# Splitting the attention values: scaled in place on ScalarE, their low halves subtracted on GpSimd from the fifth head on

## Chip, core and metric

One core of one Trainium2 chip runs the whole kernel. The metric is the device time of an execution in microseconds (us), from three timed runs; a profile of one more execution shows what each engine did.

## What is computed

Three layers follow each other. The change lies in the first.

```
# attention, 2 batches x 8 heads, 768 positions, 64 columns a head
q_bits = (q @ proj > 0); k_bits = (k @ proj > 0)      # 6 bits: a bucket for each row
mask   = q_bucket[:, None] == k_bucket[None, :]
scores = where(mask, q @ k.T / 8, -1e9)
out    = softmax(scores) @ v
# mixture of experts: 1536 tokens, each to its best of 8 experts, capacity 384
# last: g = h * clip(h + 3, 0, 6) / 6 with h = x @ w_in, and then g @ w_out
```

## The kernel before

**Precision.** Most products run in float16. A float32 number is split in two: a high half, which is the number scaled and rounded to float16, and a low half, which is the scaled number minus the high half, again rounded to float16. A product is the sum of high by high, high by low and low by high. The values `v` are split so by `vsplit(h)`, one head at a time. Their scale `s` is a power of two which the kernel finds for every group of four heads (`vmax`, `vscale`), so that scaling doesn't round.

**Attention.** The sixteen heads are cut into 96 steps, six a head, each with 128 keys and all 768 queries. For a step, `scores` makes two products on TensorE for each half of the queries, into a buffer `pst` of PSUM (L442 and L443; two such buffers), and ScalarE writes their exponentials to `pf` (L444). A step later `phi` takes the high half of `pf` (`high`, L452 on ScalarE; for a few steps L454 on VectorE), and a step after that `plo` its low half (`low`, L458, on GpSimd for steps below 84 and two later ones, otherwise on VectorE). `pv` multiplies both with the values of the head, two steps at a time, four and five steps behind the scores (L470 to L472); it reads the tile `vh` that `vsplit` writes. Eight steps ahead of the scores, `mx` makes products `psm` (L425, three buffers) of which VectorE takes the row maximum (L428).

**Around a head.** `prep` splits queries and keys (`hi` by ScalarE, L359; `lo` by VectorE, L375). `vgate` multiplies values with the expert gate on TensorE (L531) and VectorE splits the result into other columns of `vh` (L540, L541). `bits` makes the bucket bits (L398 and L387). `evac` divides a finished head by its sum (L480 to L488), and `tally` adds up the logits (L503 and L507, mostly on GpSimd).

**Order.** Nothing is scheduled by the compiler: each engine runs its instructions in the order in which the program issues them. The loop over steps issues the regular work; everything else is entered in a table `later` under a due step, and `due(k)` issues it. `spread(k, gen)` runs a generator up to its next `yield` once every step. So the first part of `vsplit(h)` is issued at step 6h plus an offset (-3.25, -4.75, -1.75 or -2.25 by the head's place in its group; heads 0 to 3 have steps of their own: 2, 3.75, 4 and 16.25), and its second part one step later. Loads of values (`load_v`) go through SyncE's queue into one of two `vr` tiles, each of which holds four heads.

**After attention.** At the end of attention the last steps' `plo`, the first expert's weight splits (`wh` by ScalarE, L157; `wl` by VectorE, L163) and the routing (`route`, `weigh`) share VectorE. Then the tokens are gathered through HBM, and the experts and the last layer follow, which the change doesn't touch.

Of the kernel before, what the change touches and what calls it, by code (L numbers as in the profile page):

```python
# [13 lines left out]
AF = mybir.ActivationFunctionType  # L14
ALU = mybir.AluOpType
# [5 lines left out]
B, H, S, D = 2, 8, 768, 64  # L21
# [19 lines left out]
VA = DE + 1  # L41
# [22 lines left out]
def moe_attention_kernel(ctx, tc, qk, v, vt, pj, wg, w1, w2, win, wout, out, cap):  # L64
    nc = tc.nc
    pe, act, dve, pool, sp = nc.tensor, nc.scalar, nc.vector, nc.gpsimd, nc.sync
# [3 lines left out]
    def opened(stack, name, bufs, side="left", **kw):  # L70
        return stack.enter_context(tc.tile_pool(name=name, bufs=bufs, side=side, reuse_waits="tile", **kw))
# [232 lines left out]
    with ExitStack() as actx:  # L304
# [361 lines left out]
        def vh(h):  # L666
            if h not in vh_t:
                vh_t[h] = pt.tile([P, NC, VW], F16, tag="vh", name=f"vh{h}", bufs=4)
            return vh_t[h]

        def vsplit(h):
            g = h // 4
            r = vr_t[g][:, h % 4]
            s = sc_t[g][:, 0:1]
            t = vh(h)
            o = E * (1 - h % 2)
            act.activation(t[:, :, o : o + D], r, AF.Copy, scale=s)
            yield
            dve.scalar_tensor_tensor(
                out=t[:, :, VA + o : VA + o + D], in0=r, scalar=s, in1=t[:, :, o : o + D],  # L680
                op0=ALU.mult, op1=ALU.subtract,
            )
            dve.memset(t[:, :, DE:VA], 1.0)

# [99 lines left out]
        for h in range(NH):  # L784
            spread(Q["v4"][h] if h < 4 else NC * h + Q["v"][h % 4], vsplit(h))
# [54 lines left out]
        h = NH - 1  # L840
# [242 lines left out]
    def heat(n):  # L1083
# [21 lines left out]
        out=gates, in0=ps2[:, :, NW:], scalar=1.0 / LS, in1=gates, op0=ALU.mult, op1=ALU.add  # L1105
# [239 lines left out]
    with ExitStack() as octx:  # L1345
        op = opened(octx, "op", 1)
# [127 lines left out]
```

## Time and profile before

| | |
|---|---|
| three runs, median | 677.33 us (677.24 to 678.81) |
| profiled execution | 675.88 us |
| its span, first to last instruction | 674.1 us |
| mean granted TensorE clock | 0.981 |
| busy over the span: TensorE, VectorE, ScalarE, GpSimd | 638.4, 481.0, 426.6, 229.8 us |
| attention | until about 240 us of the span |

The span is shorter than the execution by 1.8 us, which lie before its first and after its last instruction. Times within a trace count from the start of the span. TensorE's busy time includes matrix products that wait in its pipeline, so a busy TensorE is not one at its peak. Engines have the names PE (TensorE), PEld (its weight loads), DVE (VectorE), ACT (ScalarE), POOL (GpSimd) and SP (SyncE).

### The profile page before, as it was taken

The page shows a single profiled execution, that of the slowest core. Times are in us where ns is not written, and L with a number is a line of the kernel's source. Part 1 is how long each engine was busy: PE and PEld are TensorE (multiplying, and loading weights), DVE is VectorE, ACT ScalarE, POOL GpSimd, SP SyncE. Part 2 cuts the span into 40 slices and gives each one's busy share as a digit, 9 for nine tenths or more (in the row PEclk, how much of TensorE's full clock was granted, in tenths as well). Part 3 has the DMA queues.
Part 4 walks back from the last instruction along what each step waited for, and adds up shares of the span by engine and source line. Part 5 has one row for each costly group of instructions (what it writes and reads, how often), then busy time and mean ns, then how long its engine had stood idle before and what let it go on. Part 6 is the DMA issues. An engine that isn't in the chain of part 4 may idle for free.

```text
span 674.1 us, 14367 instructions
## 1 busy us (share of the span) xinstructions
PE 638.4 (95%) x5518; PEld 479.7 (71%) x5518; DVE 481.0 (71%) x1038; ACT 426.6 (63%) x869; POOL 229.8 (34%) x199
## 2 busy tenths in 40 slices
PE   7899999999999769999999999999999999999894
PEld 2588889989899638999999997555555555555541
DVE  6768898898999957888888877888888452222320
ACT  3467778778787826776667765455445576555730
POOL 4339769769778233221077500000000021000011
PEclk9889999999999978999999999999999999999998
DMA  8584764764465065777677735443442011000011
GB/s 236 127 233 115 231 177 122 233 169 109 126 160 165 25 217 193 250 246 257 213 253 228 243 115 162 137 145 126 150 134 92 0 48 48 1 0 1 1 41 59
DMA packets 37840, 94.14 MB, mean 140 GB/s; under 512 B 7576, under 2 KB 13720, under 8 KB 37760
## 3 DMA queue, kind: packets, MB, share of 16 engines
q1 hardware_dynamic: 34672, 85.71, 42.7%
q0 software_dynamic: 2400, 7.36, 3.2%
q8 instruction: 46, 0.75, 0.4%
q14 instruction: 34, 0.28, 0.1%
q10 hardware_dynamic: 688, 0.03, 0.1%
HBM read 67.14 MB, written 6.29 MB: 109 GB/s over the span
## 4 chain that ended last, share of the span: by engine, by line
PE 75%; DVE 10%; DMA 6%; ACT 5%; issue 2%; SPq 0%; POOL 0%; POOLq 0%; ACTq 0%; DVEq 0%
PE psg L1249 16%; PE pso L1276 15%; PE psh L1006 11%; PE psy L1033 11%; PE psm L425 5%; PE pst L442 4%; PE pst L443 3%; DVE mx L428 2%; DMA out_dram<-os,inv 2%; PE psv L470 2%; PE psv L471 2%; PE psv L472 2%; PE psg L531 2%; DMA vr<-in_v_dram 1%; ACT junk L1203 1%
## 5 line engine op out<-in xcount | busy, mean ns | idle before, releaser
L458 POOL TENSOR_TENSOR plo<-pf,phi 128x768 f16<-128x768 f32 x86 | 147.1, 1736 | 60.4 <-ACT phi L452 24.9
L444 ACT ACTIVATE pf<-pst 128x384 f32<-128x384 f32 x192 | 83.5, 486 | 47.4 <-PE pst L443 45.7
L428 DVE TENSOR_REDUCE mx<-psm 128x1 f32<-128x384 f32 x192 | 96.3, 548 | 20.0 <-PE psm L425 19.7
L1291 POOL DMA_INDIRECT out_dram<-os,inv x12 | 12.1, 1008 | 270.8 <-DVE os L1283 244.5
L163 DVE SCALAR_TENSOR_TENSOR wl<-raw,wh 128x1024 f16<-128x1024 f32 (+1 forms) x68 | 82.7, 1218 | 6.3 <-ACT wh L157 5.2
L1249 PE MATMUL psg<-yTh,ch 128*128 128x512 f16 (+1 forms) x256 | 83.4, 326 | 3.2 <-DVE rl L1252 3.2
L1249 PE MATMUL psg<-yTl,ch 128*128 128x512 f16 (+1 forms) x256 | 83.4, 326 | 0.0
L1249 PE MATMUL psg<-yTh,cl 128*128 128x512 f16 (+1 forms) x256 | 83.4, 326 | 0.0
L1252 DVE SCALAR_TENSOR_TENSOR rl<-rl,psg 128x512 f32<-128x512 f32 x64 | 35.0, 551 | 64.4 <-ACT rl L1251 64.0
L442 PE MATMUL pst<-Y,K 128*128 128x384 f32 x192 | 75.2, 392 | 2.0 <-ACT pf L444 2.0
L1249 PEld LDWEIGHTS <-ch 128*128 128x128 f16 x512 | 50.0, 98 | 35.9
L452 ACT ACTIVATE phi<-pf 128x768 f16<-128x768 f32 x85 | 71.7, 844 | 1.9
L1276 PE MATMUL pso<-ch,gh 128*128 128x512 f16 x192 | 72.8, 379 | 0.0
L1276 PE MATMUL pso<-ch,gl 128*128 128x512 f16 x192 | 72.8, 379 | 0.0
L1276 PE MATMUL pso<-cl,gh 128*128 128x512 f16 x192 | 72.8, 379 | 0.0
L425 PE MATMUL psm<-K,X 76*128 76x384 f32 x192 | 66.8, 431 | 4.6 <-DVE mx L428 3.8
L157 ACT ACTIVATE wh<-raw 128x1024 f16<-128x1024 f32 (+1 forms) x68 | 67.6, 999 | 0.5 <-issue 0.4
L1276 PEld LDWEIGHTS <-gh 128*128 128x128 f16 x384 | 37.6, 98 | 42.3
L443 PE MATMUL pst<-X,K 77*128 77x384 f32 x192 | 66.5, 346 | 0.0
L1033 PE MATMUL psy<-hh,wl 128*128 128x224 f16 x256 | 66.3, 259 | 0.0
L1033 PE MATMUL psy<-hh,wh 128*128 128x224 f16 x256 | 66.3, 259 | 0.0
L1033 PE MATMUL psy<-hl,wh 128*128 128x224 f16 x256 | 66.3, 259 | 0.0
(231 smaller groups left out, 1495.2 us busy)
## 6 DMA issues: line engine op xcount, KB each, us to landing
raw<-in_w_dram SPq DMA_DIRECT2D x64, 512.0 KB
rc<-in_win_dram SPq DMA_DIRECT2D x16, 512.0 KB
rc<-in_wout_dram SPq DMA_DIRECT2D x16, 512.0 KB
r<-in_qk_dram SPq DMA_DIRECT2D x16, 384.0 KB
K<-hi SPq DMA_DIRECT2D x31, 192.0 KB
vr<-in_v_dram SPq DMA_DIRECT2D x4, 768.0 KB
vt<-in_vt_dram SPq DMA_DIRECT2D x8, 384.0 KB
Y<-hi SPq DMA_DIRECT2D x16, 192.0 KB
```

The source lines that it names most:

```text
L163: dve.scalar_tensor_tensor(out=wl[e, i][:, c : c + n], in0=r, scalar=(S1, S2)[i // 2], in1=wh[e, i][:, c : c + n], op0=ALU.mult, op1=ALU.s ...
L425: pe.matmul(ps[:, :HS], st["X"][0:76, c::NC], st["K2"][0:76, n * HS : (n + 1) * HS], start=True, stop=True)
L428: dve.tensor_reduce(out=mm[:, c, n : n + 1], in_=ps[:, :HS], axis=AX.X, op=ALU.max)
L442: pe.matmul(ps[:, :HS], st["K1"][:, kc], st["Y"][:, qc], start=True, stop=False)
L443: pe.matmul(ps[:, :HS], st["K2"][0:77, kc], st["X"][0:77, qc], start=False, stop=True)
L444: act.activation(pf.rearrange("k (c n p) -> k c n p", c=NC, n=2)[:, :, n], ps[:, :HS].rearrange("k (p c) -> k c p", c=NC), AF.Exp, scale=0 ...
L452: act.activation(phi_t[k], pf_t[k], AF.Copy)
L458: eng.tensor_tensor(out=plo_t[k], in0=pf_t.pop(k), in1=phi_t[k], op=ALU.subtract)
L1006: pe.matmul(ps, l[:, c], r[:, k], start=n == 0, stop=n == 3 * KD - 1)
L1033: pe.matmul(ps, l, r, start=n == 0, stop=n == 3 * KF - 1)
L1249: pe.matmul(ps, l, x, start=n == 0, stop=n == 3 * KD - 1)
L1276: pe.matmul(po[blk][s], l, r, start=first and n == 0, stop=last and n == 2)
```

## The change

ScalarE scales a head's values where they lie, in the float32 tile `vr`, and then writes the high half as a copy of the scaled values. The low half is a subtraction of the high half from the scaled values, with no scale of its own. For heads 0 to 3 VectorE does it, for heads 4 to 15 GpSimd. The order of issue stays: both operations of ScalarE stand where its one stood, the subtraction where VectorE's stood, on the queue of its engine.

```diff
             o = E * (1 - h % 2)
-            act.activation(t[:, :, o : o + D], r, AF.Copy, scale=s)
-            yield
-            dve.scalar_tensor_tensor(
-                out=t[:, :, VA + o : VA + o + D], in0=r, scalar=s, in1=t[:, :, o : o + D],
-                op0=ALU.mult, op1=ALU.subtract,
+            act.activation(r, r, AF.Copy, scale=s)
+            act.activation(t[:, :, o : o + D], r, AF.Copy)
+            yield
+            eng = pool if h > 3 else dve
+            eng.tensor_tensor(
+                out=t[:, :, VA + o : VA + o + D], in0=r, in1=t[:, :, o : o + D], op=ALU.subtract
             )
             dve.memset(t[:, :, DE:VA], 1.0)
```

## Rows read from the trace of the kernel before

**Rows 1.** Busy us of each engine in a stretch (windows), with instruction counts.
```profile
60.00:220.00 160.00, 156.65 (x1905) 141.82 (x1901) 142.35 (x330) 128.04 (x239) 126.16 (x84) 1.00 0.60 165
220.00:240.00 20.00, 14.13 (x247) 11.86 (x246) 18.30 (x46) 15.36 (x34) 3.97 (x3) 1.00 0.08 23
```

**Rows 2.** Waits, 60 to 220 us: us in total, times, longest.
```profile
ACT pf L444 <- PE pst L443: 29.3, 32, 2.5
...
PEld psm L425 <- DVE mx L428: 3.9, 7, 0.6
PEld pst L442 <- ACT pf L444: 2.9, 5, 0.6
```

**Rows 3.** The chain, 119 to 124 us: start, us, what.
```profile
120.22 1.43 DVE vh L679
```

**Rows 4.** Timeline of TensorE: start, us, instruction, idle time and releaser.
```profile
123.25 0.55 PE L425 MATMUL psm<-K,X 76*128 76x384 f32 x1 [0.31 <-DVE mx L428]
```

**Rows 5.** All of L679: ns least/median/most, first and last start.
```profile
L679 DVE SCALAR_TENSOR_TENSOR vh<-vr,sc,vh x16: 606/1130/1772, 33.8 to 223.4; 128x384 f16<-128x384 f32 x16
```

**Rows 6.** Timeline of GpSimd at the same place.
```profile
117.97 3.26 POOL L458 TENSOR_TENSOR plo<-pf,phi 128x768 f16<-128x768 f32 x2
```

**Rows 7.** Timeline of VectorE at head 15.
```profile
221.73 0.69 DVE L163 SCALAR_TENSOR_TENSOR wl<-raw,wh 128x512 f16<-128x512 f32 x1
...
223.38 0.61 DVE L679 SCALAR_TENSOR_TENSOR vh<-vr,sc,vh 128x384 f16<-128x384 f32 x1
```

**Rows 8.** Timeline of GpSimd near the end of attention.
```profile
233.13 2.04 POOL L458 TENSOR_TENSOR plo<-pf,phi 128x768 f16<-128x768 f32 x1 [11.71 <-PE psv L472]
```

**Rows 9.** ScalarE's groups, 20 to 242 us: count, busy us, mean ns, idle before.
```profile
L444 ACT ACTIVATE pf<-pst 128x384 f32<-128x384 f32 x191 | 83.1, 486 | 44.5 <-PE pst L443 42.9 <-POOL plo L458 0.8
L452 ACT ACTIVATE phi<-pf 128x768 f16<-128x768 f32 x85 | 71.7, 844 | 1.9
...
L677 ACT ACTIVATE vh<-vr,sc 128x384 f16<-128x384 f32 x16 | 9.9, 622 | 1.0 <-DVE sc L594 1.0
L157 ACT ACTIVATE wh<-raw 128x512 f16<-128x512 f32 x4 | 2.5, 630 | 0.0
```

**Rows 10.** Timeline of ScalarE at heads 1 and 2.
```profile
36.46 1.11 ACT L677 ACTIVATE vh<-vr,sc 128x384 f16<-128x384 f32 x2
```

**Rows 11.** Timelines of ScalarE behind heads 7 and 8.
```profile
121.16 0.87 ACT L444 ACTIVATE pf<-pst 128x384 f32<-128x384 f32 x2 [0.57 <-PE pst L443]
...
130.69 0.87 ACT L444 ACTIVATE pf<-pst 128x384 f32<-128x384 f32 x2 [1.37 <-PE pst L443]
```

**Rows 12.** Timelines of ScalarE at head 6 and behind head 14.
```profile
105.97 0.62 ACT L677 ACTIVATE vh<-vr,sc 128x384 f16<-128x384 f32 x1
...
109.42 0.88 ACT L444 ACTIVATE pf<-pst 128x384 f32<-128x384 f32 x2
...
212.18 0.87 ACT L444 ACTIVATE pf<-pst 128x384 f32<-128x384 f32 x2
```

**Rows 13.** Timelines of TensorE at the same two places.
```profile
109.98 0.45 PE L442 MATMUL pst<-Y,K 128*128 128x384 f32 x1 [0.28 <-ACT pf L444]
...
212.74 0.43 PE L442 MATMUL pst<-Y,K 128*128 128x384 f32 x1
```

**Rows 14.** Timeline of ScalarE behind head 9.
```profile
137.93 0.85 ACT L452 ACTIVATE phi<-pf 128x768 f16<-128x768 f32 x1
138.88 0.87 ACT L444 ACTIVATE pf<-pst 128x384 f32<-128x384 f32 x2
```

**Rows 15.** All of L458 on GpSimd: ns least/median/most.
```profile
L458 POOL TENSOR_TENSOR plo<-pf,phi x86: 1632/1655/2388, 21.3 to 233.1; 128x768 f16<-128x768 f32 x86
```

**Rows 16.** GpSimd's groups, 20 to 240 us.
```profile
L503 POOL TENSOR_TENSOR lg<-xp 128x48 f32<-128x48 f32 x2 | 0.6, 282 | 2.0 <-DVE xp L488 2.0
```

**Rows 17.** Timeline of ScalarE at head 15.
```profile
221.07 0.63 ACT L157 ACTIVATE wh<-raw 128x512 f16<-128x512 f32 x1
```

**Rows 18.** All of L375 on VectorE: ns least/median/most.
```profile
L375 DVE SCALAR_TENSOR_TENSOR lo<-r,hi x15: 947/999/2031, 20.6 to 200.3; 128x768 fp32r<-128x768 f32 x15
```

## Prediction

> **What bounds the kernel now.** The change touches attention alone, whose steady part lies between 60 and 220 us, so I began with the busy time by stretch. In the steady part [rows 1] TensorE is busy 156.65 of 160 us, VectorE 142.35, ScalarE 128.04 and GpSimd 126.16; in the last 20 us of attention VectorE has 18.30 of 20 and GpSimd hardly works. TensorE sets the pace first, VectorE at the end. VectorE's busy time in the steady part is then worth no more than the time for which it stops TensorE.
>
> The waits answer that [rows 2]. TensorE's weight loads waited seven times for `mx` (L428), VectorE's row maximum, 3.9 us in all or 0.56 us each, and five times for `pf` (L444), ScalarE's exponential, 2.9 us in all or 0.58 us each. No wait there names the low half of the values, `vh` on L679. It stands in VectorE's queue ahead of maxima that are awaited, and so it comes up on the chain [rows 3]: 1.43 us of it until 121.65, short scale operations and one maximum behind it, and the `psm` product (L425) that waited for this maximum starts at 123.25 [rows 4].
>
> **Part one: VectorE loses L679 for twelve heads.** It takes 606 ns at best, 1130 in the median and 1772 at worst [rows 5]. GpSimd makes the difference: the operation of the chain came while GpSimd's `plo` ran until 121.23 [rows 6], and the one at 223.38 with GpSimd idle took 0.61 us [rows 7, 8]. Twelve operations of about 1.2 us, some 14 us, leave VectorE. Heads 0 to 3 keep theirs there as a plain subtraction of the same operands; I cost that difference at nothing, since of these four only head 3's is followed by a stall and its length is set by GpSimd.
>
> What is bought is stalls. Of the seven, one follows head 3's operation, which stays, and one at 204 us stands behind routing work with no L679 close ahead. Five come within 8 us of an L679 that leaves: near 84 (head 4), 123 (head 7, the row shown), 136 (head 8), 175 and 179 us (head 11). Each is about 0.56 us deep and some 1.4 us [rows 3] come out of the queue ahead of it, so I let all five close: 5 x 0.56 = 2.8 us. The bounds are 0 (something else holds the maxima up) and 6 x 0.6 = 3.6 us (the one at 204 goes too, each as long as the longest).
>
> **Part two: ScalarE gains an operation for all sixteen heads.** L677 takes 622 ns for 384 columns with the scale read from a tile [rows 9]; the added copy has none. L452 and L157 are such operations, 844 ns for 768 columns and 630 for 512: 0.836 ns a column, 523 ns for 384. Two L677 in a row took 1.11 us [rows 10], so independent operations overlap by some 0.11. The copy reads what the first one wrote, and I let the first run to its end: it gives up an overlap of 0.11 in front of the copy, and the copy overlaps its follower by as much, so 0.523 us is added a head. Bounds are 0.41 (they overlap) and 0.62 (as long as L677).
>
> Behind it in ScalarE's queue are `phi` (L452) and the next `pf`, and TensorE's scores need the `pst` buffer that `pf` frees. Where ScalarE waits for TensorE anyway the addition costs nothing: at heads 3, 7 and 11 that wait is 0.57 us some 3 us later, at 4, 8 and 12 more than a microsecond [rows 11]. Heads 0 to 2 lie in the start, where ScalarE pauses for TensorE too: of 42.9 us of such pauses between 20 and 242 us [rows 9], 29.3 lie in the steady part [rows 2]. At heads 6, 10 and 13 there is none: ScalarE goes without a break from `vh` through `phi`, `pf`, `hi` to the `pf` at 109.42 [rows 12], and TensorE stops for that one [rows 13]. At head 14 it is unbroken too, and the product at 212.74 starts just as the buffer of the `pf` from 212.18 comes free [rows 12, 13]. At these four the whole addition is lost: 4 x 0.52 = 2.1 us (bounds 1.6 and 2.5). At heads 5 and 9 ScalarE pauses for only 0.1 us [rows 14], but TensorE was late there by the stall that part one closes. With that gone ScalarE is the later one; I take back 0.2 us at each, 0.4 us.
>
> **Part three: GpSimd gains a subtraction for twelve heads.** Its subtraction takes 1655 ns for 768 columns and 282 for 48 [rows 15, 16], 1.91 ns a column, so about 0.92 us for 384. Eleven of them lie in the steady part, 10 us, which takes GpSimd from 126 to 136 of 160 us. Queued behind each are later `plo`. The value products want a `plo` two to three steps after it is issued, and a step is 2.1 us (15 heads of 6 steps between the first and the last L679 [rows 5]). TensorE has no wait on GpSimd among those of the steady part, and one subtraction in six steps doesn't fill that distance, so I cost it at nothing; without this cover it is 0.92 us a head at most. No DMA is moved. The load that overwrites the second group of values now waits for head 7's subtraction on GpSimd, as early in the program as before.
>
> The GPSIMD Engine Reference of the Trainium skill, under "Engine selection", puts elementwise work of two inputs on VectorE, GpSimd being about twice as slow for it. The rows agree in kind (0.92 against 0.61 us). Here the slower engine has idle time and the faster one has not, and the sum doesn't use the rule.
>
> **Part four: the end.** Head 15's operation lies where VectorE itself is the chain. On ScalarE `vh` is followed at once by `wh` (L157), which ends at 221.70, and VectorE's `wl` (L163), which reads it, starts at 221.73 [rows 7, 17]. The addition delays `wl` by 0.52 us; 1.6 us later VectorE saves 0.55 us of L679. GpSimd is idle there [rows 8] and starts its subtraction at about 221.7, until 222.6; `wl`, then due at 222.25, may be held until that end, 0.35 us. Together about +0.3 us, between -0.6 (only the saving) and +0.9 (held for a whole subtraction).
>
> **The sum.** -2.8 + 0.4 + 2.1 + 0.3 = 0.0 us. The profiled execution took 675.88 us and would take the same; the median of the three runs, 677.33, stands 1.45 us above it, so the forecast is 677.3 us. What a measurement of this kernel can tell from no change is about 0.3%, or 2.0 us.
>
> **The rivals.** First, ScalarE becomes the bound: slower. With VectorE's stalls gone TensorE asks for each `pf` sooner, and ScalarE's pauses are used up. Heads 5, 6, 9, 10, 13 and 14 lose 0.62 us each, 3.7 us, the end loses 0.9, and of the gains three stalls at heads 7 and 11 remain, 1.7 us: +2.9 us, 680.2. It decides once the addition exceeds the pause ahead of `pf` in six heads rather than four. Against it speak 29.3 us of such pauses [rows 2], 0.9 us each; for it, that they are bunched and two heads have 0.1 us.
>
> Second, the relief reaches farther: faster. Six stalls of 0.6 us close, ScalarE's price is 0.41 us at four heads, and the end saves 0.6: -3.6 + 1.6 - 0.6 = -2.6 us, 674.7. For it speak the 14 us that leave an engine busy for 89% of the stretch; against it, that TensorE stands hardly longer than the two waits of [rows 2] say.
>
> Third, the subtraction only moves the contention: slower. GpSimd's operations now hold up what stays on VectorE with two inputs in SBUF, `lo` (L375) above all, which takes 947 ns at best and 2031 at worst [rows 18], and the maxima are as late as before. Nothing is gained, and 2.1 + 0.3 = +2.4 us is left, 679.7. Against it: GpSimd's busy time grows by 8% only, and so should the lengthening. The same page lists, under "Specifications", that GpSimd shares its SBUF interfaces with VectorE and contends with VectorE instructions of two SBUF inputs; the spread of L679 agrees.
>
> **How the numbers follow.** Forecast 0.50, ScalarE as bound 0.17, farther relief 0.18, moved contention 0.15. The forecast's own range is 675.7 to 678.9, from the bounds of its terms against each other. The whole range reaches to the outer rivals, 674.4 to 680.4, and leaves about a tenth at each side. Faster by over 2.0 us is most of the second rival and a little of the forecast, 0.20. Slower is most of the first, two thirds of the third and very little of the forecast, 0.25. Within is 0.55.
>
> **What would show it.** Part one: VectorE's busy time between 60 and 220 us falls by some 13 us, waits of weight loads on `mx` fall from seven to about two, and nothing of L679's kind stands on the chain after head 3. Part two: a copy of 0.52 us behind each scaling, and waits on `pf` of about 1.1 us at heads 6, 10 and 13. Part three: GpSimd operations of 0.92 us, and no wait of TensorE on `plo` before 220 us. Part four: `wl` 0.5 us later against the `pf` ahead of it. The forecast is wrong if the subtraction on GpSimd takes far more than 0.92 us, since value products would then wait for `plo`; if the five stalls have another cause than the queue behind L679; or if ScalarE's addition shows at more heads than four.

## The result and the profile after

The changed kernel took 682.16 us (median of 12 runs, 679.13 to 685.11) beside 676.36 us for the kernel before in the same session: a ratio of 1.0077, 95% interval 1.0051 to 1.0102, so 5.2 us slower (3.5 to 6.9). The forecast was 677.3 us with a range of 674.4 to 680.4. The profiled execution of the changed kernel took 679.92 us, its span is 677.9.

Lines move by the edit: the scaling in place is L677, the new copy L678, the subtraction L681, the memset L684. First the busy time by stretch in the changed kernel (busy us and instruction counts of TensorE, its weight loads, VectorE, ScalarE and GpSimd, then TensorE's granted clock, the DMA share, GB/s), which answers to [rows 1]:

```profile
60.00:220.00 160.00, 152.91 (x1836) 138.06 (x1835) 134.31 (x305) 129.42 (x244) 130.87 (x93) 0.98 0.60 164
...
84.00:88.00 4.00, 3.94 (x54) 2.97 (x54) 3.74 (x4) 3.97 (x9) 4.00 (x4) 1.00 0.64 154
88.00:92.00 4.00, 1.07 (x5) 0.73 (x5) 4.00 (x1) 1.77 (x4) 3.34 (x3) 1.00 0.22 61
92.00:96.00 4.00, 3.32 (x41) 2.76 (x45) 2.73 (x8) 0.00 (x0) 0.00 (x0) 0.50 0.62 177
96.00:100.00 4.00, 4.00 (x20) 2.97 (x12) 2.57 (x7) 1.80 (x4) 0.29 (x1) 0.65 0.09 26
100.00:104.00 4.00, 4.00 (x53) 3.64 (x53) 3.27 (x7) 3.44 (x8) 3.27 (x2) 1.00 0.65 182
```

VectorE lost 8 us of work in the steady part, yet TensorE did less too: 1836 products instead of 1905. The damage has one place. Between 88 and 92 us TensorE works 1.07 of 4 us while VectorE is busy all the time with one instruction. From 92 us on TensorE runs for four microseconds at a granted clock of 0.50, its lower level of 1.2 GHz, and for four more at 0.65. The kernel before in two of these stretches:

```profile
88.00:92.00 4.00, 4.00 (x60) 2.90 (x53) 3.12 (x8) 1.51 (x3) 3.08 (x3) 1.00 0.78 197
92.00:96.00 4.00, 4.00 (x50) 3.70 (x50) 3.93 (x10) 3.21 (x6) 1.28 (x2) 1.00 0.65 196
```

The waits of the steady part say the same beside [rows 2] (total, times, longest):

```profile
ACT pf L444 <- PE pst L443: 28.2, 26, 8.3
...
PEld psm L425 <- DVE mx L428: 4.8, 3, 3.9
PEld pst L442 <- ACT pf L444: 4.7, 5, 1.1
PE psm L425 <- DVE mx L428: 4.2, 2, 3.6
```

Seven waits on `mx` of about 0.56 us have become three, and one of them alone is 3.9 us long. The five on `pf` grew from 0.6 to 1.1 us at the longest. The one instruction is head 6's `lo` (L375). These are the timelines of the changed kernel there, VectorE first, then GpSimd, then TensorE (start, us, instruction, idle time and releaser):

```profile
84.33 1.02 DVE L428 TENSOR_REDUCE mx<-psm 128x1 f32<-128x384 f32 x2 [0.26 <-PE psm L425]
85.27 6.89 DVE L375 SCALAR_TENSOR_TENSOR lo<-r,hi 128x768 fp32r<-128x768 f32 x1
92.08 1.01 DVE L428 TENSOR_REDUCE mx<-psm 128x1 f32<-128x384 f32 x2
```

```profile
80.54 6.49 POOL L458 TENSOR_TENSOR plo<-pf,phi 128x768 f16<-128x768 f32 x4
87.00 0.89 POOL L681 TENSOR_TENSOR vh<-vr,vh 128x384 f16<-128x384 f32 x1
87.85 3.24 POOL L458 TENSOR_TENSOR plo<-pf,phi 128x768 f16<-128x768 f32 x2
91.06 0.28 POOL L507 TENSOR_TENSOR lg<-xp,lg 128x48 f32<-128x48 f32 x1
```

```profile
88.68 0.39 PE L425 MATMUL psm<-K,X 76*128 76x384 f32 x1
92.68 0.70 PE L425 MATMUL psm<-K,X 76*128 76x384 f32 x1 [3.60 <-DVE mx L428]
```

GpSimd runs these eight operations without a pause from 80.54 to 91.34 us; head 5's new subtraction is the fifth. `lo` starts as the third of them ends, is passed over at every change of operation and ends at 92.16, 0.82 us after GpSimd falls idle. It takes 6.89 us where [rows 18] had 2.03 at most. The maxima queued behind it come that late, the `psm` product waits for them, and after 3.60 us of standing still TensorE has the lower clock. In the kernel before, the same `lo` took:

```profile
85.83 1.57 DVE L375 SCALAR_TENSOR_TENSOR lo<-r,hi 128x768 fp32r<-128x768 f32 x1
```

GpSimd paused there for 0.34 us, and `lo` ended 0.8 us after the pause began:

```profile
86.93 3.91 POOL L458 TENSOR_TENSOR plo<-pf,phi 128x768 f16<-128x768 f32 x2 [0.34 <-PE pst L443]
```

The price can be worked out from the windows: 3.6 us of standing, and at most 4 x 0.50 + 4 x 0.35 = 3.4 us lost to the clock in the eight microseconds behind it, 7.0 us together. In the traces the scores of step 26 (counted from 0) start 0.61 us earlier than before, those of step 29 5.97 us later and those of step 32 5.72 us later: 6.3 to 6.6 us lost at this place.

The SBUF — State Buffer page of the Trainium skill ("SBUF: two separate sides") states that the interface shared by GpSimd and VectorE is an exclusive lock, held for a whole instruction, and that the loser waits entirely. The trace agrees in that `lo` hardly advances while GpSimd works: 6.89 us, against 0.95 us for the same instruction at its shortest. It shows one thing more: the wait lasts over five instructions of GpSimd that started after `lo` had, not over one.

The new and moved lines, all instances of each in the changed kernel (ns least, median, most, first and last start):

```profile
L677 ACT ACTIVATE vr<-vr,sc x16: 600/616/634, 25.3 to 225.7; 128x384 f32<-128x384 f32 x16
...
L678 ACT ACTIVATE vh<-vr x16: 527/530/532, 26.0 to 226.3; 128x384 f16<-128x384 f32 x16
...
L681 POOL TENSOR_TENSOR vh<-vr,vh x12: 886/893/1553, 79.7 to 226.9; 128x384 f16<-128x384 f32 x12
L681 DVE TENSOR_TENSOR vh<-vr,vh x4: 543/1032/1736, 33.8 to 68.0; 128x384 f16<-128x384 f32 x4
...
L375 DVE SCALAR_TENSOR_TENSOR lo<-r,hi x15: 948/1242/6887, 20.8 to 205.6; 128x768 fp32r<-128x768 f32 x15
```

The copy (0.53 us) and the subtraction (0.89 us) cost what the prediction gave them (0.52 and 0.92). At heads 6, 10 and 13 the stall on `pf` grew as foreseen; TensorE's timeline of the changed kernel, where the kernel before has 0.27 to 0.28 us of idle time at the three places ([rows 13] show the first):

```profile
116.26 0.44 PE L442 MATMUL pst<-Y,K 128*128 128x384 f32 x1 [0.77 <-ACT pf L444]
...
167.63 0.44 PE L442 MATMUL pst<-Y,K 128*128 128x384 f32 x1 [0.77 <-ACT pf L444]
...
196.92 0.45 PE L442 MATMUL pst<-Y,K 128*128 128x384 f32 x1 [0.84 <-ACT pf L444]
```

### The profile page after: what moved, and what is told of

It is laid out like the page before. It is cut to its first block, busy times and chain, and to the rows that moved or that the text cites. A ratio compares the mean times of both kernels' runs of the same rounds, so it can differ in the third digit from the quotient of the medians.

```text
span 677.9 us, 14387 instructions
## 1 busy us (share of the span) xinstructions
PE 637.5 (94%) x5518; PEld 478.6 (71%) x5518; DVE 479.6 (71%) x1026; ACT 434.0 (64%) x885; POOL 238.3 (35%) x211
## 4 chain that ended last, share of the span: by engine, by line
PE 77%; DVE 9%; DMA 5%; ACT 5%; issue 3%; SPq 0%; POOL 0%; POOLq 0%; DVEq 0%; ACTq 0%
PE psg L1250 16%; PE pso L1277 15%; PE psy L1034 11%; PE psh L1007 10%; PE psm L425 5%; PE pst L442 5%; PE pst L443 4%; DMA out_dram<-os,inv 2%; PE psv L470 2%; PE psv L471 2%; PE psv L472 2%; DVE mx L428 2%; ACT junk L1204 1%; PE psb L398 1%; PE psg L531 1%
## 5 line engine op out<-in xcount | busy, mean ns | idle before, releaser
L458 POOL TENSOR_TENSOR plo<-pf,phi 128x768 f16<-128x768 f32 x86 | 143.4, 1690 | 54.5 <-ACT phi L452 22.0
L444 ACT ACTIVATE pf<-pst 128x384 f32<-128x384 f32 x192 | 83.2, 483 | 47.0 <-PE pst L443 46.0
L163 DVE SCALAR_TENSOR_TENSOR wl<-raw,wh 128x1024 f16<-128x1024 f32 (+1 forms) x68 | 83.1, 1224 | 6.3 <-ACT wh L157 5.8
L425 PE MATMUL psm<-K,X 76*128 76x384 f32 x192 | 65.4, 426 | 7.3 <-DVE mx L428 6.5
L157 ACT ACTIVATE wh<-raw 128x1024 f16<-128x1024 f32 (+1 forms) x68 | 67.6, 998 | 0.9 <-DVE offs L889 0.9
```

The source lines that it names most:

```text
L163: dve.scalar_tensor_tensor(out=wl[e, i][:, c : c + n], in0=r, scalar=(S1, S2)[i // 2], in1=wh[e, i][:, c : c + n], op0=ALU.mult, op1=ALU.s ...
L425: pe.matmul(ps[:, :HS], st["X"][0:76, c::NC], st["K2"][0:76, n * HS : (n + 1) * HS], start=True, stop=True)
L444: act.activation(pf.rearrange("k (c n p) -> k c n p", c=NC, n=2)[:, :, n], ps[:, :HS].rearrange("k (p c) -> k c p", c=NC), AF.Exp, scale=0 ...
L458: eng.tensor_tensor(out=plo_t[k], in0=pf_t.pop(k), in1=phi_t[k], op=ALU.subtract)
```

## The experiments

The theories keep the letters that the expectations give them. Ratios are to the kernel before in the same session, with 95% intervals.

**The changed kernel again.** No edit; is the long `lo` a chance of one execution?

> The changed kernel once more. In its first profile VectorE's lo (L375) that starts at 85.27 us takes 6.89 us, while GpSimd runs five operations without a pause, head 5's new subtraction among them. Theory A (GpSimd's unbroken chain shuts VectorE's two-input operation out, set up by the fixed order): lo takes over 5 us at the same place again, and attention ends 5 to 6 us later than before. Theory B (the 6.89 us were chance, and ScalarE's added copies cost the time): no lo over 2.4 us, and the time is still 4 to 6 us above before. Ratio to before 1.005 to 1.010 by both.

Measured: 681.82 us, ratio 1.0081 (1.0058 to 1.0105). In another profiled execution `lo` starts at 85.42 and takes 6.86 us. It belongs to the kernel. The last exponential of attention (L444) starts 6.8 us later than in the kernel before, 5.4 us later in the first trace of the changed kernel.

**ScalarE's part alone.** All sixteen subtractions on VectorE.

```
-            eng = pool if h > 3 else dve
+            eng = dve
```

> The subtraction stays on VectorE for all heads; scaling in place and the added copy on ScalarE stay. Theory A: no lo over 2.4 us; what is left is ScalarE's price without the relief, by the prediction's terms 2.1 us at four heads and 0.5 us at the end, so 1 to 3 us above before. Theory B: 4 to 6 us above before, as the changed kernel.

Measured: 680.0 us, ratio 1.0053 (1.0027 to 1.0080), and the longest `lo` takes 2.05 us. What is left of the change, ScalarE's added copies and the plain subtractions that wait for them, costs 3.6 us (1.8 to 5.4). This lies between the times that the two theories gave; the missing long `lo` is what speaks for theory A.

**All but head 5.** One subtraction of twelve goes back to VectorE.

```
-            eng = pool if h > 3 else dve
+            eng = pool if h > 3 and h != 5 else dve
```

> As the changed kernel, but head 5's subtraction back on VectorE. Theory A: the lo at 85 us takes at most 2.3 us and the time is 5 to 6 us below the changed kernel, within 1.5 us of before. Theory B: within 1 us of the changed kernel, 4 to 6 us above before.

Measured: 675.48 us, ratio 0.998 (0.9952 to 1.0008), 6.3 us below the changed kernel on the same chip. The rows there, VectorE and then GpSimd:

```profile
86.00 2.58 DVE L375 SCALAR_TENSOR_TENSOR lo<-r,hi 128x768 fp32r<-128x768 f32 x1
```

```profile
82.86 4.90 POOL L458 TENSOR_TENSOR plo<-pf,phi 128x768 f16<-128x768 f32 x3
88.28 3.75 POOL L458 TENSOR_TENSOR plo<-pf,phi 128x768 f16<-128x768 f32 x2 [0.51 <-ACT phi L452]
```

`lo` is passed over once, then GpSimd runs out of work for 0.51 us and `lo` gets in. One subtraction made the whole loss.

**Head 5 alone.**

```
-            eng = pool if h > 3 else dve
+            eng = pool if h == 5 else dve
```

> Only head 5's subtraction on GpSimd, all others on VectorE. Theory A: the lo near 85 us takes over 5 us, and the time is 5 to 8 us above before (the shut-out with ScalarE's price and without the relief). Theory B: as with all subtractions on VectorE, within 1 us of it.

Measured: 680.03 us, ratio 1.0054 (1.0033 to 1.0075), and `lo` takes 1.57 us. The expectation that the event would come with this subtraction alone was wrong: the changed kernel does not lose without it, but it does not make the loss by itself. GpSimd reached it at 86.97 us after a pause of 0.12 us, when `lo` was already in its turn. The time equals that of the version with no subtraction on GpSimd.

**`lo` a little later.** A VectorE memset of 256 columns ahead of head 6's `lo`, in the changed kernel.

```
+            if h == 6:
+                dve.memset(nud, 0.0)
```

> The changed kernel with one clearing of 256 float32 columns, about 0.27 us, ahead of head 6's lo on VectorE; GpSimd's five operations stay as they are. Theory A1 (lo is shut out because it asks within some 0.15 us of the handover from one GpSimd operation to the next): asked 0.25 us later, lo gets in at the next handover, takes at most 2.4 us, and the time falls by 5 to 6 us, to within 1.5 us of before. Theory A2 (any lo that meets an unbroken chain of GpSimd operations waits for its end): lo still ends near 92 us, lasting over 6 us, and the time stays 5 to 6 us above before.

Measured: 683.6 us, ratio 1.0093 (1.0060 to 1.0125). `lo` now starts at 87.43, after GpSimd's change of operation at 87.25 and not just ahead of one, and still takes 6.59 us. It is no coincidence of two starts within 0.15 us.

**Head 5's subtraction a step later.**

```
             yield
+            if h == 5:
+                yield
             eng = pool if h > 3 else dve
```

> The changed kernel with head 5's subtraction issued one step later, lo as early as in the changed kernel. Theory A (head 5's subtraction fills the pause of GpSimd in which VectorE got in): the pause comes back, lo takes at most 2.6 us, as with head 5 on VectorE, and the time is within 1.5 us of before. If the number of operations alone counted (theory A0, more GpSimd work, more contention): within 1 us of the changed kernel.

Measured: 677.08 us, ratio 1.0013 (0.9988 to 1.0038); `lo` takes 2.56 us. All twelve subtractions are on GpSimd, all copies on ScalarE, and only the place of one in GpSimd's queue differs: 4.6 us by the two ratios.

**The relief alone.** The new form at heads 4, 7, 8 and 11, where VectorE's operation was followed by a stall, the old form at the other twelve.

```
+            if h in (4, 7, 8, 11):
+                act.activation(r, r, AF.Copy, scale=s)
+                act.activation(t[:, :, o : o + D], r, AF.Copy)
+                yield
+                pool.tensor_tensor(out=lo, in0=r, in1=t[:, :, o : o + D], op=ALU.subtract)
+            else:
...
```

> The new form at heads 4, 7, 8 and 11 only, those that stand ahead of the five stalls; all others as before. By the prediction's terms the relief of 2.8 us stays and ScalarE's price at heads 6, 10, 13, 14 and 15 goes: 2 to 3.5 us below before, ratio about 0.996. Rival (the relief needs the whole 14 us taken from VectorE): within 1 us of before.

Measured: 673.76 us, ratio 0.9957 (0.9931 to 0.9984): 2.9 us faster than before (1.1 to 4.7), and faster than the changed kernel. The waits from 60 to 220 us in this version:

```profile
PEld pst L442 <- ACT pf L444: 3.1, 6, 0.6
...
PEld psm L425 <- DVE mx L428: 0.8, 2, 0.6
```

The waits on `mx` of [rows 2] go from 3.9 to 0.8 us, those on `pf` hardly move.

**Eleven heads** (4 and 6 to 15 new; 0 to 3 and 5 old).

```
-            if h in (4, 7, 8, 11):
+            if h in (4, 6, 7, 8, 9, 10, 11, 12, 13, 14, 15):
```

> The new form at heads 4 and 6 to 15; heads 0 to 3 and 5 as before. Against the run with head 5's subtraction on VectorE it lacks the added copies at heads 0 to 3 and 5. If these copies are free, as the prediction has them, within 1 us of that run (ratio to before 0.998); if they cost in the start, 1 to 2 us below it.

Measured: 676.69 us, ratio 1.0008 (0.9984 to 1.0033), `lo` 2.55 us. This is 1.1 us above the run with all but head 5, measured from each session's kernel before, which fits neither of the two outcomes given; the intervals overlap, so the added copies at heads 0 to 3 and 5 cannot be seen in the time. Of those at the other heads some use up what the relief brings.

**A filler on GpSimd in the kernel before.** A subtraction of 128x384 on scratch tiles, read by nobody, ahead of step 9, and in a second kernel ahead of step 16.

```
+                if u == 9:
+                    pool.tensor_tensor(out=fo[:, :, 0:D], in0=fa, in1=fb, op=ALU.subtract)
                 low(u, pool if on_pool(u) else dve)
```

> The kernel before with one more operation on GpSimd, a subtraction of 128x384 on scratch tiles (0.9 us, it waits for nothing), ahead of the tenth plo, near 54 us; nothing else is changed. Theory R (GpSimd keeps VectorE's lo out at every handover for which its next operation was released 0.3 us or more ahead; it lets lo in where that was 0.2 us or less): the filler puts GpSimd 0.9 us further behind its inputs, each plo is then released about 1 us ahead, and the lo that starts at 58.4 us in the kernel before takes 4 to 7 us instead of 1.33; 3 to 6 us above before. Rival (the shut-out needs the changed kernel's own operations: values scaled in place, a subtraction that reads what ScalarE wrote): lo takes at most 2.4 us, within 1 us of before.

> The same filler ahead of the seventeenth plo, near 67.6 us, where GpSimd then stands idle for 3.9 us before VectorE's next lo is over. Theory R: no lo over 2.4 us, within 1 us of before. Rival (0.9 us more of GpSimd's work costs wherever it lies): as with the filler near 54 us.

Measured: 677.18 us, ratio 1.0012 (0.9991 to 1.0034), and 677.07 us, ratio 1.0005 (0.9987 to 1.0023). The first missed its expectation and tests little: the `lo` aimed at came when GpSimd was idle (59.84 to 61.92 us). The second came out as expected: 0.9 us more on GpSimd as such costs nothing.

**Five heads** (3, 4, 7, 8 and 11).

> The new form at heads 3, 4, 7, 8 and 11. Head 3's operation stands ahead of the stall at 71 us, and ScalarE waits 0.54 us there. By the terms of the prediction 0.5 us below the version with four heads, so 3 to 3.5 us below before, ratio about 0.995. Rival: GpSimd's added work near 68 us delays the lo at 71.6 us, and nothing or a loss against four heads comes of it.

Measured: 673.92 us, ratio 0.9962 (0.9942 to 0.9982): the same as with four. The 0.5 us expected beyond it is too little for these intervals to show.

**The filler at head 5's place,** ahead of step 25, in the kernel before.

```
-                if u == 9:
+                if u == 25:
```

> The kernel before with one more GpSimd operation: a subtraction of 128x384 on scratch tiles, which waits for nothing and so can start as soon as GpSimd has done what stands ahead of it, put where the changed kernel has head 5's (near 87 us, with head 6's lo on VectorE). It computes nothing that the output uses. Theory R (a VectorE lo of two wide inputs stays out as long as GpSimd's next operation has been free to start well before the last one ends, and a subtraction there that is free early puts GpSimd behind, so that the operations behind it are free early too): lo takes 4 to 7 us, and the time is 4 to 6 us above before. Rival (it needs something else of the changed kernel, the copies or the scaled values): lo takes at most 2.6 us, and the time is within 1 us of before, as with the same filler at the two other places.

Measured: 677.35 us, ratio 1.0006 (0.9981 to 1.0031). `lo` was not shut out:

```profile
86.81 1.56 DVE L380 SCALAR_TENSOR_TENSOR lo<-r,hi 128x768 fp32r<-128x768 f32 x1
```

```profile
85.90 1.65 POOL L463 TENSOR_TENSOR plo<-pf,phi 128x768 f16<-128x768 f32 x1
87.51 1.64 POOL L828 TENSOR_TENSOR fo<-fa,fb 128x384 f16<-128x384 f32 x1
```

Here the filler was made to wait (1.64 us instead of 0.9) and `lo` had its turn, though the filler waits for nothing. So theory R, which went by that time alone, fell. GpSimd had paused 0.1 us right ahead of the operation at 85.90, so it was not behind with its work.

**`lo` a pair of maxima earlier,** in the changed kernel.

```
-            spread(NC * h + Q["pr"][h % 4], prep(h), Q["prd"])
+            spread(NC * h + Q["pr"][h % 4], prep(h), 0.5 if h == 6 else Q["prd"])
```

> The changed kernel with head 6's lo given to VectorE one pair of mx earlier (its step 0.5 instead of 0.6 after hi), so that it asks near 84.2 us instead of 85.3, before the third of GpSimd's five operations in a row is free to start (84.9 us). Theory F (GpSimd keeps its turn when its next operation was free to start before lo asked; an lo that asks first gets the next turn): lo ends 0.8 us after the operation that runs when it asks, takes 1.2 to 2.2 us, and the time is back within 1.5 us of before. Theory R (an operation that is free 0.3 us or more before the one ahead of it ends shuts lo out, whoever asked first): lo still ends only when GpSimd falls idle, takes 6 to 8.5 us, and the time is 4 to 7 us above before.

Measured: 685.51 us (four runs, 682.34 to 689.35), ratio 1.0107 (1.0058 to 1.0155). `lo` starts at 84.48 and takes 7.97 us, until 0.82 us after GpSimd's last operation (91.36 + 0.27). Asking first does not help, theory F fell here:

```profile
84.48 7.97 DVE L375 SCALAR_TENSOR_TENSOR lo<-r,hi 128x768 fp32r<-128x768 f32 x1
```

`lo` came as theory R has it, and the time is 7.2 us above before by the ratio, just past the 4 to 7 of that theory. The profiled execution is the longest of the four. Its trace holds a second event of the kind, at head 14's subtraction, and what is kept out there is a routing operation of two inputs of 6 columns (L247), which takes 0.16 to 0.31 us at this place in every other trace. VectorE, GpSimd (without a pause since 210.41 us), TensorE:

```profile
218.24 4.37 DVE L247 SCALAR_TENSOR_TENSOR pl<-mx,pos 128x6 f32<-128x6 f32 x1
```

```profile
218.47 0.91 POOL L681 TENSOR_TENSOR vh<-vr,vh 128x384 f16<-128x384 f32 x1
219.31 3.27 POOL L458 TENSOR_TENSOR plo<-pf,phi 128x768 f16<-128x768 f32 x2
```

```profile
223.22 0.70 PE L425 MATMUL psm<-K,X 76*128 76x384 f32 x1 [2.14 <-DVE mx L428]
```

It ends 0.03 us after GpSimd's last operation, and TensorE stood for 2.14 us. So the shut-out does not need a wide operation, nor head 5's place. Whether it needs head 14's subtraction no run tested; in the other traces of the changed kernel the same operation got in here.

**Filler at step 25 and `lo` later,** in the kernel before: the edits of two runs above together.

> The kernel before with the filler of the run before it (a GpSimd subtraction on scratch tiles that waits for nothing, ahead of step 25) and a VectorE memset of 256 columns ahead of head 6's lo, so that lo asks some 0.3 us later, clearly after the filler is free to start. Theory F: lo loses the turn to the filler, and as GpSimd is then behind, loses the next ones too: 3 to 7 us, and the time 2 to 6 us above before. Rival (operations on scratch tiles do not shut lo out, as without the memset): lo takes 1.2 to 2.6 us, and the time is within 1 us of before.

Measured: 677.99 us, ratio 1.0028 (1.0004 to 1.0053). `lo` takes 1.29 us, against theory F again; the rival's numbers came, but not for its reason, as the next run shows. GpSimd had a pause right ahead, as without the memset.

**The filler in the version with four heads,** where GpSimd runs without a pause up to head 6's `lo`, at the place of head 5's subtraction, which this version keeps on VectorE.

```
+                if u == 25:
+                    pool.tensor_tensor(out=fo[:, :, 0:D], in0=fa, in1=fb, op=ALU.subtract)
                 low(u, pool if on_pool(u) else dve)
```

> The version with the new form at heads 4, 7, 8 and 11 alone, with the filler (a GpSimd subtraction on scratch tiles that waits for nothing) ahead of step 25, where the changed kernel has head 5's subtraction. GpSimd runs without a pause there, as in the changed kernel, and lo of head 6 loses one turn there already (2.58 us without the filler). If any operation of 0.9 us that is free early in that place shuts lo out (none of head 5's copies or data needed): lo takes 4 to 8 us, and the time is 4 to 6 us above the same version without the filler, near 678.5 us where before is 676.5. Rival (it needs head 5's own operations): lo takes at most 3.5 us, and the time is within 1.5 us of the same version without the filler, near 674.

Measured: 680.06 us, ratio 1.0077 (1.0046 to 1.0108). By medians this is 6.3 us above the same version without the filler, of which 0.4 us is the difference between the two sessions' kernel before. VectorE's row, and GpSimd's:

```profile
85.27 6.90 DVE L380 SCALAR_TENSOR_TENSOR lo<-r,hi 128x768 fp32r<-128x768 f32 x1
```

```profile
80.53 6.49 POOL L463 TENSOR_TENSOR plo<-pf,phi 128x768 f16<-128x768 f32 x4
86.99 0.92 POOL L834 TENSOR_TENSOR fo<-fa,fb 128x384 f16<-128x384 f32 x1
87.86 3.25 POOL L463 TENSOR_TENSOR plo<-pf,phi 128x768 f16<-128x768 f32 x2
91.06 0.29 POOL L512 TENSOR_TENSOR lg<-xp,lg 128x48 f32<-128x48 f32 x1
```

This is the changed kernel's picture to within 0.02 us, made by an operation that computes nothing. What shuts `lo` out is one more GpSimd operation at this place while GpSimd runs without a pause, not head 5's data, copies or wait.

## Why the prediction was wrong

**Part one** held. The stalls on `mx` at heads 4, 7, 8 and 11 closed, with nothing of L679's kind behind them, and the version with these four heads gains 2.9 us (1.1 to 4.7) where the prediction put 2.8. In the changed kernel the stall at 204 us, which the sum had left in place, shrank as well (0.63 to 0.16 us). VectorE's own busy time fell by 8.0 us rather than 13, since one `lo` took 5.3 us more than before.

**Part two** held in the main. The stalls behind heads 6, 10 and 13 are there and no others of that size. Start by start, ScalarE's exponentials (L444) in the trace with all but head 5's subtraction fall behind those of the kernel before by 0.56 to 0.58 us at each of these three heads, where 0.52 was put; at head 14, where 0.52 was put too, they gain 0.53 us by the stall at 204 and lose 0.40 again, so that its price can't be read by itself. Without the relief the copies cost 3.6 us (1.8 to 5.4), where the prediction put 2.1 for the steady part and 0.5 for the delay of `wl`; the 0.4 at heads 5 and 9 was not due in that run, since VectorE's stalls stayed.

**Part four** held in its mechanism. In the changed kernel's timelines of ScalarE, GpSimd and VectorE at head 15, `wl` (L163) starts when `wh` (L157) ends and runs on beside GpSimd's subtraction:

```profile
226.32 0.53 ACT L678 ACTIVATE vh<-vr 128x384 f16<-128x384 f32 x1
226.75 0.61 ACT L157 ACTIVATE wh<-raw 128x512 f16<-128x512 f32 x1
```

```profile
226.93 0.89 POOL L681 TENSOR_TENSOR vh<-vr,vh 128x384 f16<-128x384 f32 x1 [0.38 <-ACT vh L678]
```

```profile
227.40 0.97 DVE L163 SCALAR_TENSOR_TENSOR wl<-raw,wh 128x512 f16<-128x512 f32 x1 [0.60 <-ACT wh L157]
```

It took 0.97 us instead of the 0.69 of [rows 7], held by 0.28 us where 0.35 was put.

**Part three failed**: the subtraction "cost at nothing". It looked for the price in what GpSimd delivers, a late `plo`, and there it was right, for no wait on `plo` by TensorE appeared. The price was in what GpSimd keeps from VectorE. The third rival named the mechanism and the instruction, `lo` (L375) above all, but sized it as an average: busy time on GpSimd grows by 8%, "and so should the lengthening". It is no average. Eleven of the twelve subtractions cost nothing that the time shows, and the rest of the sum came out with them: with head 5's taken off GpSimd the ratio is 0.998 (0.9952 to 1.0008), with it a step later 1.0013 (0.9988 to 1.0038), both around the forecast's sum of 0.0. The twelfth lengthened one `lo` by 5.3 us over its time before, which cost 4.6 to 6.3 us by the three comparisons (head 5's subtraction taken off GpSimd, put a step later, or replaced by a filler); by the windows about half of that is the stall and half the lower clock behind it.

GpSimd's 126.16 of 160 us in [rows 1] could not show it. The run with all but head 5's subtraction has 133.66 us there, more than the changed kernel's 130.87, and loses nothing. What counts is not that share but whether GpSimd always has its next operation ready while a VectorE operation of two SBUF inputs waits, and a timeline around each `lo` is where to look for it. In the changed kernel GpSimd runs from 73.22 to 91.34 us without a pause; without head 5's subtraction the stretch breaks off at 87.77 us, after `lo` has been passed over once.

**Left open** is how the turn is given. Take GpSimd's next operation as free when the operation whose result it reads has ended. In these traces a `lo` that waits gets in wherever this was 0.24 us or less before the one ahead on GpSimd ended, with a pause or without one (in the version with four heads at 0.19 us, without a pause). It stayed out where it was 0.33 us or more and GpSimd had not paused; the two fillers behind a pause wait for nothing, and `lo` got in. Width does not order it: the values' own operations of 384 columns got in at 0.14 to 1.15 us, the one of 6 columns stayed out at 0.29 to 0.42. This fits all runs, but it was read out of them afterwards and no run tested it by itself.

## What to carry to other kernels

Before GpSimd is given one more operation, look at each stretch in which it would then run without a pause, and at which VectorE operation of two SBUF inputs, wide or not, falls into it: that one can be kept out until GpSimd runs dry, and everything queued behind it is as late. The cost is not proportional to the work moved; one of twelve operations made the loss, and the same operation a step later cost nothing that could be measured. Move work only where the trace shows a stall behind it: four heads of sixteen gave 2.9 us, sixteen gave a loss.

## What the runs showed of the hardware

A VectorE operation of two inputs of 768 columns, 0.95 us by itself, took 6.59 to 7.97 us beside GpSimd operations in a row, four or five of which started while it waited, and ended 0.81 to 0.82 us after the last of them in each of these runs: it did hardly any of its work before. One of 6 columns, 0.16 to 0.31 us otherwise, took 4.37 us in the same way. TensorE, after 3.60 us without work, was granted 0.50 of its clock over the next 4 us and 0.65 over the 4 after, so that this stall cost nearly twice its length (6.3 to 6.6 us by the starts of the scores).
